# The second token weight kept in row order: no staging, no Pool copies, a stepped read in the matmul, and late z turns queued early

## Chip, cores, metric

One core of a Trainium2 chip. The time is the device time of one execution in microseconds (us), quoted as a median of several. This program runs on one core, so a run is marked slow by its time alone, when it lies over 1.5% above the fastest of its kernel. The granted clock is TensorE's clock as a share of full speed.

## The reference

Eight batches of 3008 tokens by 256 channels. An attention without softmax, a gate by `u`, and then a two-part mixer:

```python
scores = (1 / S) * (z @ z.T)                  # z: [8, 3008, 64]
attn   = np.maximum(scores, 0) ** 2
x      = u * (attn @ v)                       # [8, 3008, 256]
h      = np.maximum(x.T @ w_tok1, 0) @ w_tok2 # w_tok2: [256, 3008]
u2     = x + h.T
out    = u2 + np.maximum(u2 @ w_ch1, 0) @ w_ch2
```

## The kernel before

S = 3008 tokens are taken in six groups of QW = 512 (the last has 448: three full tiles of 128, and a rest of 64). Inside a group, partition p holds n = 4 neighbouring tokens (3 in the last group), so that the loads have long runs. All that is laid along the tokens inside the kernel (`uT`, `acc`, `xT`) therefore has the order "tile t, partition s", while the weight `w_tok2` comes from memory in the order "s, t". Before, Pool brings it into the kernel's order:

```python
def load_w_tok2(c):
    st = sb.tile([P, DT, QW], BF16, tag="h2", name="ws", bufs=ROOM["h2"])
    W = widths[c]
    nc.gpsimd.dma_start(out=st[:, :, :W], in_=...[:, :, c * QW:c * QW + W])
    ...
def order_w_tok2(c):
    ...
    for h in range(DT):
        nc.gpsimd.tensor_copy(
            w_tok2_sb[:, h, c * QW:c * QW + n * P].rearrange("p (t s) -> p t s", s=P),
            st[:, h, :n * P].rearrange("p (s t) -> p t s", t=n))
    if n * P < W:
        nc.gpsimd.tensor_copy(w_tok2_sb[:, :, c * QW + n * P:c * QW + W], st[:, :, n * P:W])
```

The matmul that uses it, and VectorE's addition behind it. The third argument of `matmul`, here the weight, is called the moving operand below, and a column is one of its elements in each partition, 512 or 448 in this kernel; its tile lies in SBUF. `h_ps` lies in PSUM, where this kernel puts the results of its matmuls, with room for 512 fp32 columns for each of two channel halves:

```python
def tok2(q, end):
    ...
    for dh in range(DT):
        for th in range(2):
            nc.tensor.matmul(
                h[:, dh, :W], st["a"][:, th, dh * P:(dh + 1) * P],
                w_tok2_sb[:, th, q * QW:q * QW + W], start=(th == 0), stop=(th == 1))
    def add(t):
        nc.vector.tensor_add(xT[:, :, :W], xT[:, :, :W], h[:, :, :W])
        ...
```

In each attention block VectorE squares the scores (`square`, one instruction for each pair of score tiles) and, at the end of a block, multiplies the two accumulator halves by `uT` (`gate`, one instruction for each half; this is the hand-over that frees the accumulators for TensorE). After the second gate the block's `xT` is turned by a DMA transpose into `x_sb`:

```python
def square(unit, view, t):
    nc.vector.tensor_mul(view, view, view)
    ...
def gate(blk, dh, t):
    ...
    nc.vector.tensor_mul(xT[:, dh, ...], acc[...], uT[:, :full, dh, :])
    ...
    if dh == DT - 1:
        push("sp", t, 1.25, 7.5, lambda t: turn_x(b, q, t), first=1)   # DMA transpose x_sb <- xT
```

The program is written by a scheduler that models the engines' times and decides in which order each engine's instructions are emitted. In the first batch the last two of six groups of `z` are doubled by VectorE and turned by TensorE in the middle of the first block:

```python
def turn_late_z(c):
    zr = double_first_z(c)
    ...
    turn_on_pe(zr, zp)
    ...
for c in range(GK, NG):
    at_group(c - GK + 1, lambda c=c: turn_late_z(c))
```

## Time and profile before

| | before |
|---|---|
| median of three runs | 1175.21 us (1170.55 to 1176.49) |
| profiled span, granted clock | 1168.6 us, 0.999 |
| TensorE busy, matmuls | 1159.7 us, 7049 |
| `h_ps` matmuls | 192, worth 40.6 us at the pace of the chain |
| Pool's 13 ordering copies | 9.0 us, once in the program |

How to read it: TensorE is busy for all but 9 us, so what counts of a matmul is its **pace**, the distance from one to the next in the chain. The lines of the profile stand in the prediction below.

### The profile page before, as it was taken

What the parts mean: (1) busy time and instruction counts of PE and PEld (TensorE: products, weight loads), DVE (VectorE), ACT (ScalarE), POOL (GpSimd) and SP (SyncE); (2) the same over time, 40 slices, a digit from 0 to 9 for tenths busy, and PEclk for the clock granted to TensorE, in tenths of its full rate; (3) what the DMA queues carried; (4) which work ended last, traced back from release to release, by engine and by line L of the source; (5) the groups of instructions that cost most, each with busy time, mean ns of one, the idle gap of its engine ahead of it and who ended that gap; (6) DMA issues with size and microseconds to landing.
All of it is one profiled execution on the core that took longest, in us unless ns stands there. A gap on an engine that the chain in (4) does not pass through costs nothing.

```text
span 1168.6 us, 17791 instructions
## 1 busy us (share of the span) xinstructions
PE 1159.7 (99%) x7049; PEld 630.0 (54%) x7049; DVE 541.8 (46%) x819; ACT 521.4 (45%) x650; POOL 158.3 (14%) x328
## 2 busy tenths in 40 slices
PE   9999999999999999999999999999999999999998
PEld 3334554655546555555555655465454655555666
DVE  5785653355333563435634355242552336512544
ACT  7877443244442363343524435344454344513221
POOL 4462001102012100120101210101201000000000
PEclk9999999999999999999999999999999999999999
DMA  9999737997497965896758986798667977632121
GB/s 166 186 157 197 173 92 149 162 190 132 117 167 152 168 132 134 145 181 147 145 131 163 166 152 125 138 186 156 122 141 140 187 145 151 121 100 58 50 82 64
DMA packets 472883, 165.57 MB, mean 142 GB/s; under 512 B 436640, under 2 KB 450528, under 8 KB 472800
## 3 DMA queue, kind: packets, MB, share of 16 engines
q1 hardware_dynamic: 444944, 131.74, 53.6%
q0 software_dynamic: 27344, 32.32, 19.8%
q8 instruction: 55, 0.90, 0.3%
q10 hardware_dynamic: 512, 0.38, 0.1%
q14 instruction: 28, 0.23, 0.1%
HBM read 65.40 MB, written 24.64 MB: 77 GB/s over the span
## 4 chain that ended last, share of the span: by engine, by line
PE 93%; DMA 3%; DVE 2%; POOL 1%; issue 1%; ACT 0%; SPq 0%; ACTq 0%; DVEq 0%; POOLq 0%
PE acc L533 39%; PE op L771 21%; PE hp L729 21%; PE sc L399 6%; PE a_ps L675 4%; PE h_ps L692 3%; DVE at L445 1%; DMA zT<-zr 1%; DMA ur<-in_u_dram 1%; DMA fl<-at 0%; DMA uT<-ur 0%; DMA zf<-in_z_dram 0%; DVE xT L628 0%; ACT at L437 0%; DVE xT L698 0%
## 5 line engine op out<-in xcount | busy, mean ns | idle before, releaser
L742 ACT ACTIVATE h2pre<-hp 128x1024 bf16<-128x1024 f32 (+1 forms) x191 | 191.0, 1006 | 364.5 <-PE hp L729 363.4
L533 PEld LDWEIGHTS <-v_sb 128*128 128x128 bf16 (+1 forms) x2304 | 209.6, 98 | 267.1 <-issue 65.1
L533 PE MATMUL acc<-at,v_sb 128*128 128x512 bf16 (+3 forms) x1464 | 350.7, 378 | 1.9 <-DVE xT L628 1.3
L437 ACT ACTIVATE at<-sc 128x1024 bf16<-128x1024 f32 (+1 forms) x284 | 272.0, 1024 | 159.4 <-PE sc L399 156.1
L445 DVE TENSOR_TENSOR at<-at 128x1024 bf16<-128x1024 bf16 (+1 forms) x284 | 200.7, 716 | 174.3 <-ACT at L437 174.1
L729 PE MATMUL hp<-xT,w_ch_sb 128*128 128x512 bf16 (+1 forms) x1152 | 266.7, 375 | 0.0
L771 PE MATMUL op<-w_ch_sb,h2pre 128*128 128x256 bf16 x2208 | 258.4, 273 | 0.3 <-DVE xT L698 0.2
L771 PEld LDWEIGHTS <-h2pre 128*128 128x128 bf16 x2208 | 215.9, 98 | 46.1 <-issue 0.5
L533 PE MATMUL acc<-fl,v_sb 128*128 128x512 bf16 (+1 forms) x840 | 199.9, 371 | 0.0
L729 PEld LDWEIGHTS <-w_ch_sb 128*128 128x128 bf16 x1152 | 112.7, 98 | 126.8 <-issue 0.2
L784 DVE TENSOR_TENSOR res<-op,u_sb 128x512 f32<-128x512 f32 x87 | 60.1, 691 | 206.5 <-PE op L771 206.5
L744 DVE TENSOR_SCALAR h2pre<-hp 128x1024 bf16<-128x1024 f32 (+1 forms) x97 | 117.3, 1209 | 52.4 <-PE hp L729 51.5
L628 DVE TENSOR_TENSOR xT<-acc,uT 128x512 bf16<-128x512 f32 (+1 forms) x96 | 63.2, 665 | 114.0 <-PE acc L533 113.6
L399 PE MATMUL sc<-zT 64*128 64x512 bf16 (+1 forms) x732 | 95.2, 361 | 0.3
L425 ACT ACTIVATE at<-sc 128x512 bf16<-128x512 f32 (+3 forms) x164 | 59.2, 446 | 67.7 <-PE sc L399 67.5
L125 POOL COPY zr<-zs 128x512 bf16<-128x512 bf16 x42 | 26.1, 623 | 399.6 <-DMA zT<-zr 393.9
L473 DVE TENSOR_TENSOR at<-at 128x512 bf16<-128x512 bf16 (+3 forms) x164 | 44.3, 324 | 59.2 <-ACT at L425 59.2
L399 PEld LDWEIGHTS <-zT 64*128 64x128 bf16 x732 | 31.2, 94 | 56.8 <-issue 39.8
L698 DVE TENSOR_TENSOR xT<-xT,h_ps 128x1024 bf16<-128x1024 bf16 (+1 forms) x48 | 55.6, 1191 | 6.4 <-PE h_ps L692 6.3
L168 POOL DMA_DIRECT2D v_sb<-in_v_dram x48 | 25.9, 545 | 143.7 <-PE acc L533 142.4
L675 PE MATMUL a_ps<-x_sb,w_tok_sb 128*128 128x256 bf16 x384 | 44.7, 273 | 0.0
L692 PE MATMUL h_ps<-w_tok_sb,a_sb 128*128 128x512 bf16 (+1 forms) x192 | 44.5, 374 | 0.1
(43 smaller groups left out, 209.9 us busy)
## 6 DMA issues: line engine op xcount, KB each, us to landing
out_dram<-res SPq DMA_DIRECT2D x87, 256.0 KB, 2.2
v_sb<-in_v_dram POOLq DMA_DIRECT2D x40, 256.0 KB, 4.9
ur<-in_u_dram POOLq DMA_DIRECT2D x40, 256.0 KB, 5.1
zs<-in_z_dram POOLq DMA_DIRECT2D x35, 64.0 KB, 4.4
at<-at SPq DMA_TRANSPOSE x123, 2.4
fl<-at SPq DMA_TRANSPOSE x105, 3.9
v_sb<-in_v_dram POOLq DMA_DIRECT2D x8, 192.0 KB, 6.3
ur<-in_u_dram POOLq DMA_DIRECT2D x8, 192.0 KB, 5.6
```

Source lines behind the costliest of these rows:

```text
L399: nc.tensor.matmul(sc[:, r, c0:c1], zT[h, k * P:(k + 1) * P], zT[h, q * QW + c0:q * QW + c1], start=True, stop=True)
L437: nc.scalar.activation(view, sv, ACT.Relu, scale=inv_S)
L445: nc.vector.tensor_mul(view, view, view)
L533: nc.tensor.matmul(o, vs[blk.b, g][rows, i, dh * P:(dh + 1) * P], rhs, start=first, stop=stop, skip_group_check=True)
L628: nc.vector.tensor_mul(xT[:, dh, :full * P].rearrange("p (t s) -> p t s", s=P), acc[:, :full * P].rearrange("p (t s) -> p t s", s=P), uT[: ...
L675: nc.tensor.matmul(st["a_ps"][:, th, :], w_tok1_sb[:, k, th * P:(th + 1) * P], x[:, :, i, :], start=(k == 0 and th == 0), stop=(k == KT - ...
L692: nc.tensor.matmul(h[:, dh, :W], st["a"][:, th, dh * P:(dh + 1) * P], w_tok2_sb[:, th, q * QW:q * QW + W], start=(th == 0), stop=(th == 1))
L729: nc.tensor.matmul(hp[:, r, :W], w_ch1_sb[:, dc, cc * P:(cc + 1) * P], xT[:, dc, :W], start=(dc == 0), stop=(dc == DT - 1))
L742: nc.scalar.activation(h2[:, :, :W], hp[:, :, :W], ACT.Relu)
L744: nc.vector.tensor_single_scalar(h2[:, :, :W], hp[:, :, :W], 0.0, AX.max)
L771: nc.tensor.matmul(op[:, i, :], h2, w_ch2_sb[:, cc, :], start=(cc == 0 and (i == 0 or apart)), stop=(cc == CHT - 1), skip_group_check=True)
L784: nc.vector.tensor_add(res.rearrange("p i (h d) -> p i h d", d=P), op.rearrange("p i (h d) -> p i h d", d=P), us[:, :, half * 2:half * 2 + ...
```

## The change

The intent: keep the weight as it comes, load it straight into its place, and let the matmul's moving operand pick every fourth element (every third in the last group). That drops the staging tiles and the copies. Because the 384 stepped columns and the rest of 64 don't form one regular pattern, the last group's matmul is split into 384 and 64 columns. Along with it the late `z` turns become pieces that are queued at the start and taken as soon as they are ready.

```diff
     def load_w_tok2(c):
-        st = sb.tile([P, DT, QW], BF16, tag="h2", name="ws", bufs=ROOM["h2"])
         W = widths[c]
         nc.gpsimd.dma_start(
-            out=st[:, :, :W],
+            out=w_tok2_sb[:, :, c * QW:c * QW + W],
             in_=...
-    def order_w_tok2(c):
-        ...                                   # the Pool copies shown above
@@ tok2
+                    a = st["a"][:, th, dh * P:(dh + 1) * P]
+                    w = w_tok2_sb[:, th, q * QW:q * QW + W]
                     nc.tensor.matmul(
-                        h[:, dh, :W], st["a"][:, th, dh * P:(dh + 1) * P],
-                        w_tok2_sb[:, th, q * QW:q * QW + W], start=(th == 0), stop=(th == 1))
+                        h[:, dh, :n * P].rearrange("p (t s) -> p t s", s=P), a,
+                        w[:, :n * P].rearrange("p (s t) -> p t s", t=n),
+                        start=(th == 0), stop=(th == 1), skip_group_check=True)
+                    if n * P < W:
+                        nc.tensor.matmul(
+                            h[:, dh, n * P:W], a, w[:, n * P:], start=False,
+                            stop=(th == 1), skip_group_check=True)
@@ late z
-    def turn_late_z(c):
-        ...
-    for c in range(GK, NG):
-        at_group(c - GK + 1, lambda c=c: turn_late_z(c))
+    def late_z(c, landed):
+        zr = []
+        def turn(end):
+            ...
+            turn_on_pe(zr[0], zp)
+            ...
+        cast = push("dve", landed, 0.42, 0.55, lambda t: zr.append(double_first_z(c)))
+        heads.append(Piece(0.23, [cast], turn, urgent=True))
...
     score_run(units[:2], 5.3)
+    late_z(4, 7.8)
+    late_z(5, 9.0)
```

More of the change, by code (lines that the diff above doesn't have):

```diff
@@ L45, with __init__ @@
 class Piece:
-    def __init__(self, cost, needs, fn, opens=False, closes=False, room=None):
+    def __init__(self, cost, needs, fn, opens=False, closes=False, room=None,
+                 urgent=False):
         self.cost, self.needs, self.fn = cost, needs, fn
         self.opens, self.closes, self.room = opens, closes, room
+        self.urgent = urgent
 @with_exitstack
@@ L205, in load_w_tok2 @@
     def load_w_tok2(c):
-        st = sb.tile([P, DT, QW], BF16, tag="h2", name="ws", bufs=ROOM["h2"])
         W = widths[c]
         nc.gpsimd.dma_start(
-            out=st[:, :, :W],
+            out=w_tok2_sb[:, :, c * QW:c * QW + W],
             in_=moe_w_tok2.rearrange("(tc t) s -> t tc s", t=P)[:, :, c * QW:c * QW + W])
-        ws[c] = st
-        live["h2"] += 1
         loading(LOAD)
-    def order_w_tok2(c):
-        st = ws.pop(c)
-        live["h2"] -= 1
-        W, n = widths[c], full_tiles[c]
-        for h in range(DT):
-            nc.gpsimd.tensor_copy(
-                w_tok2_sb[:, h, c * QW:c * QW + n * P].rearrange("p (t s) -> p t s", s=P),
-                st[:, h, :n * P].rearrange("p (s t) -> p t s", t=n))
-        if n * P < W:
-            nc.gpsimd.tensor_copy(
-                w_tok2_sb[:, :, c * QW + n * P:c * QW + W], st[:, :, n * P:W])
     def load_w_ch(part):
@@ L237, in load_w_ch @@
         loading(LOAD * 1.5)
-    zTs, vs, urs, uTs, xTs, xs, ws = {}, {}, {}, {}, {}, {}, {}
+    zTs, vs, urs, uTs, xTs, xs = {}, {}, {}, {}, {}, {}
     attn = {}
@@ L689, in tok2 @@
             h = psum.tile([P, DT, QW], F32, tag="ps", name="h_ps", bufs=3)
+            n = full_tiles[q]
             for dh in range(DT):
                 for th in range(2):
+                    a = st["a"][:, th, dh * P:(dh + 1) * P]
+                    w = w_tok2_sb[:, th, q * QW:q * QW + W]
                     nc.tensor.matmul(
-                        h[:, dh, :W], st["a"][:, th, dh * P:(dh + 1) * P],
-                        w_tok2_sb[:, th, q * QW:q * QW + W], start=(th == 0), stop=(th == 1))
+                        h[:, dh, :n * P].rearrange("p (t s) -> p t s", s=P), a,
[5 more added lines that the diff above has]
+                            stop=(th == 1), skip_group_check=True)
             def add(t):
@@ L938 @@
                              lambda b=b, c=c: load_v(b + 1, c))
-    def turn_late_z(c):
-        zr = double_first_z(c)
-        free["dve"] = max(free["dve"], pe[0]) + 0.45
-        while all(d.t is None for d in ring):
-            run_engines(next_op()[0][0])
-        begin = max(free["dve"] + 0.1, min(d.t for d in ring if d.t is not None))
-        take_slot()
-        begin, end = on_pe(max(pe[0], begin), "full", 0.23)
-        zp = psum.tile([P, GK, P], F32, tag="ps", name="zp", bufs=3)
-        turn_on_pe(zr, zp)
-        turned[0, c] = Done()
-        ring.append(push(
-            "dve", end + 0.1, 0.66, 0.8,
-            lambda t: nc.vector.tensor_copy(zTs[0][:, c * GK:c * GK + GK, :], zp[:]),
-            first=1, done=turned[0, c]))
-    for c in range(GK, NG):
-        at_group(c - GK + 1, lambda c=c: turn_late_z(c))
+    def late_z(c, landed):
+        zr = []
+        def turn(end):
+            take_slot()
+            zp = psum.tile([P, GK, P], F32, tag="ps", name="zp", bufs=3)
+            turn_on_pe(zr[0], zp)
+            turned[0, c] = Done()
+            ring.append(push(
+                "dve", end + 0.2, 0.66, 0.8,
+                lambda t: nc.vector.tensor_copy(zTs[0][:, c * GK:c * GK + GK, :], zp[:]),
+                first=1, done=turned[0, c]))
+        cast = push("dve", landed, 0.42, 0.55, lambda t: zr.append(double_first_z(c)))
+        heads.append(Piece(0.23, [cast], turn, urgent=True))
     at_group(3, lambda: turn_u(0, 0))
@@ L969 @@
     items += [lambda c=c: load_w_tok1(c) for c in range(NG)]
-    first_tok2 = len(items)
     items += [lambda c=c: load_w_tok2(c) for c in range(NG)]
@@ L975 @@
         at_group(n, item)
-        if 0 <= k - first_tok2 < NG:
-            at_group(n + 4, lambda c=k - first_tok2: order_w_tok2(c))
     per_batch = 0.87 * NQ * (2 + CHT // 2) + 1.35 * 4 * NQ
@@ L1037 @@
             pick, n_now, ts = "scores", now, t
+        elif tm <= t + NOW and pieces[0].urgent:
+            pick = "mixer"
         elif hold and opened[0] is not None and tm <= t + NOW and pieces is opened[0]:
@@ L1075 @@
         else:
-            budget -= pieces[0].cost
+            if not pieces[0].urgent:
+                budget -= pieces[0].cost
             do_piece(tm, pieces)
```

## The prediction

> **What bounds the kernel now.** I read the page first, its busy times and its chain of waits, then the groups by line, then the stretches where the chain leaves TensorE.
>
> ```profile
> PE 1159.7 (99%) x7049; PEld 630.0 (54%) x7049; DVE 541.8 (46%) x819; ACT 521.4 (45%) x650; POOL 158.3 (14%) x328
> PE 93%; DMA 3%; DVE 2%; POOL 1%; issue 1%; ACT 0%; SPq 0%; ACTq 0%; DVEq 0%; POOLq 0%
> PE acc L533 39%; PE op L771 21%; PE hp L729 21%; PE sc L399 6%; PE a_ps L675 4%; PE h_ps L692 3%; DVE at L445 1%; DMA zT<-zr 1%; DMA ur<-in_u_dram 1%; DMA fl<-at 0%; DMA uT<-ur 0%; DMA zf<-in_z_dram 0%; DVE xT L628 0%; ACT at L437 0%; DVE xT L698 0%
> ```
>
> TensorE is busy 99% of 1168.6 us and carries 93% of the chain. So every nanosecond put into a matmul is paid in full, and a nanosecond taken from Pool or VectorE is worth something only in the few places where TensorE waits for them. The granted clock is 0.999, so no throttle is in play. The operation that the change touches is h_ps, 3% of the span. The groups by line:
>
> ```profile
> L692 PE MATMUL h_ps<-w_tok_sb,a_sb 128*128 128x512 bf16 (+1 forms) x192 | 44.5, 374 | 0.1
> L698 DVE TENSOR_TENSOR xT<-xT,h_ps 128x1024 bf16<-128x1024 bf16 (+1 forms) x48 | 55.6, 1191 | 6.4 <-PE h_ps L692 6.3
> L220 POOL COPY w_tok_sb<-ws 128x512 bf16<-128x512 bf16 (+1 forms) x12 | 8.7, 755 | 1.0 <-DMA ws<-in_moe_w_tok_dram 1.0
> L125 POOL COPY zr<-zs 128x512 bf16<-128x512 bf16 x42 | 26.1, 623 | 399.6 <-DMA zT<-zr 393.9 <-DMA zs<-in_z_dram 5.5
> ```
>
> 374 ns is the latency of one matmul, with its overlap. What it costs is its pace, which the chain in order of time gives:
>
> ```profile
> 115.86 2.59 PE h_ps L692 x12
> 263.43 0.76 PE h_ps L692 x4
> ```
>
> So 2.59/12 = 0.216 us for 512 columns and 0.76/4 = 0.19 us for 448. All of h_ps is 160 x 0.216 + 32 x 0.19 = 40.6 us.
>
> Pool is idle most of the time, but its copies are not quite harmless. In the only stretch where L220 runs (67.2 to 80.2 us) the chain goes through VectorE; first the chain, then the group in that stretch, then the timeline:
>
> ```profile
> 67.61 11.41 DVE at L445 x11
> 79.02 0.24 issue
> 79.26 1.74 DVE at L445
> 81.00 0.61 DVE xT L628
> ```
> ```profile
> L445 DVE TENSOR_TENSOR at<-at x13: 612/1062/2387, 65.7 to 79.3; 128x1024 bf16<-128x1024 bf16 x8, 128x896 bf16<-128x896 bf16 x5
> ```
> ```profile
> 81.66 2.73 PE L533 MATMUL acc<-at,v_sb 128*128 128x448 bf16 x14 [0.72 <-DVE xT L628]
> ```
>
> L445, the square, has a median of 692 ns over the whole run and 1062 ns here, once 2387 ns. VectorE falls behind, the gate that frees the accumulator comes late, and TensorE waits for it, but only 0.72 us. That is the whole visible price of the staging.
>
> The start is the other place. Two z groups are cast by VectorE and turned by TensorE in the middle of the first block (first fence, the timeline), and the block's end hangs on a transfer (second fence, the chain):
>
> ```profile
> 11.11 0.23 PEld L149 LDWEIGHTS <-zr 128*128 128x128 bf16 x4 [0.93 <-DVE zr L143]
> 11.12 0.40 PE L149 MATMUL zp<-ident,zr 128*128 128x128 bf16 x4 [0.43 <-DVE zr L143]
> 15.53 0.40 PE L149 MATMUL zp<-ident,zr 128*128 128x128 bf16 x4 [0.25 <-DVE zr L143]
> ```
> ```profile
> 11.67 6.98 DMA ur<-in_u_dram
> 18.65 0.02 issue
> 18.66 5.78 DMA uT<-ur
> 24.45 0.03 issue
> 24.48 0.02 DVEq L628
> 24.50 0.04 issue
> 24.54 0.70 DVE xT L628
> 25.24 0.04 issue
> 25.29 0.81 PE acc L533 x3
> ```
>
> [...] The new read steps 4 bf16 = 8 bytes (3 = 6 bytes in the last group)[...]. No matmul of this trace steps its moving operand between neighbouring elements[...]. Pool reads with this very step in L220: the two 128x384 copies took 521 ns each, where the unit-step 128x512 copies of L125 have a median of 613 and the 128x128 copies of L749 a mean of 296; a line through those two gives about 507 ns at 384 columns. So no penalty on Pool, at a lower rate of elements. [...] the 692 ns squares become 1062 beside L220. [...]
>
> **The change, part by part.**
>
> Removed, Pool copies: 13 copies, 9.0 us of Pool, once in the program and not per batch. Worth on the path: the 0.72 us wait at 81.66. Estimate -0.7 us. The six loads stay, with the same bytes and the same runs; only the target differs.
>
> Removed, staging tiles: six buffers of the pool of eight, all during the first batch, when the mixer that shares them hasn't begun. No wait on them is seen. Zero.
>
> Moved, the late z turns: the casts are queued at the start and the turns are taken as soon as they are ready. The waits that vanish are 0.43 + 0.25 = 0.68 us. TensorE is idle 1.51 us between 5.6 and 25.3 us (19.70 less 18.19 busy). But the block can't hand over before uT has landed at 24.45 and the gate has run; TensorE's own last matmuls of that block ended near 24.3, so both arrive together. What TensorE gains earlier it mostly waits for at 25.29. I take half of the 0.68, -0.3 us.
>
> Added, the split tail: in the last group 448 columns become 384 + 64, so 4 more pairs of weight load and matmul per batch, 32 in all. The four turning pairs above go at 0.23/4 = 57 ns a pair with 128 columns, so a pair with 64 columns costs at most about that, against 64/448 x 190 = 27 ns of the stream that it takes over: +30 ns x 32 = +1.0 us.
>
> Changed, the moving read: 192 matmuls, the 160 full ones and 32 of 384 columns. If the stride is free, 0. If it halves the rate, these 192 take twice their 160 x 0.216 + 32 x 0.163 = 39.8 us, so +39.8 us, none of it hidden, since TensorE is the bound; VectorE's add behind each group of four (1.19 us) would then be shorter than the 1.73 us of the matmuls and hide.
>
> Sum with a free stride: -0.7 - 0.3 + 1.0 + 0 = 0.0 us, so 1175 us, the median of before.
>
> **Rivals.** First, the stride costs. A rate of one half gives 1175 + 40 = 1215 us, slower by 3.4%; a loss of a quarter of the rate (a third more time) gives 1188. For it speaks that TensorE takes 512 elements in 0.216 us, 2.4 in a nanosecond, twice what the line through the copies of Pool gives (1.2)[...]. [...] I give full cost 12% and partial cost 10%.
>
> Second, the start is worth more. If ScalarE, no longer starved (it waits 4.3 us for scores between 5 and 26 us), runs ahead so far that the second block goes without gaps, all of the 1.51 us and some of the filling matmuls come back, and the copies' end gives a little more: 1172 us. Against it stands uT at 24.45, which the change doesn't touch[...].
>
> Third, the order of emission shifts. The program orders its pieces by a model of the engines' times, and an earlier start can reorder score runs and mixer pieces in later batches. Each wait that can arise is under a microsecond; I allow 3 us either way, the same size as the spread of before's runs (1170.55 to 1176.49).
>
> **Range and chances.** With a free stride (78%) the sum of the small terms and the spread gives 1168 to 1180. Partial cost reaches from 1180 to 1200, full cost lies near 1215. A range of 1166 to 1190 holds the first case and half of the second. Faster by over 2% would need 23 us out of a kernel whose TensorE is idle 9 us in all: 1%. Slower by over 2% starts at 1199, so it takes the full cost or nearly: 16%. Within 2%: 83%.
>
> **What would show it right or wrong.** The pace of h_ps in the chain: 2.59 us for 12 means that the stride is free, 5.2 that it is halved. Squares near 67 to 80 us back at 0.69 us, and the 0.72 us wait at the gate gone. The first block's hand-over still near 25 us, with uT as its releaser. Matmuls up by 32, to 7081 or a few others by the filling ones. The prediction is wrong if h_ps's matmuls keep TensorE longer than 42 us, or if the hand-over of the first block moves by over 2 us.

## The result, and the profile after

The change costs 52 us. Before had a median of 1173.02 us (1170.55 to 1176.49, 4 runs), after 1221.68 us (1221.67 to 1225.04, 4 runs); the ratio is 1.042, interval 1.0382 to 1.0457, outside the predicted range of 1166 to 1190. All ratios in this document compare fast runs of the same rounds, so they are not quite the ratio of the medians. All results are correct unless said otherwise.

The page of after, its busy times and the chain by line:

```profile
PE 1203.4 (99%) x7081; PEld 635.4 (52%) x7081; DVE 540.0 (44%) x819; ACT 521.6 (43%) x650; POOL 150.5 (12%) x315
...
PE acc L521 39%; PE op L767 20%; PE hp L725 20%; PE h_ps L683 7%; PE sc L387 6%; PE a_ps L663 4%; DMA fl<-at 1%; DMA ur<-in_u_dram 1%; DMA zf<-in_z_dram 0%; DMA uT<-ur 0%; ACT at L425 0%; POOL v_sb L170 0%; SPq L480 0%; DVE xT L616 0%; SPq L628 0%
```

The profiled span went from 1168.6 to 1219.9 us, by 51.3. TensorE's busy time went up by 43.7 us (1159.7 to 1203.4) and its idle time by 7.6 (8.9 to 16.5). `h_ps` has gone from 3% to 7% of the span, and `DMA fl<-at` from 0% to 1%. So there are **two costs**: most of it is work, some of it is waiting. The matmuls are 7081, the predicted 32 more, and Pool has its 13 copies less.

The work first. The chain of after in order of time; the columns are start, length, what, how many:

```profile
127.23 5.42 PE h_ps L683 x12
...
139.05 2.06 PE h_ps L683 x5
141.11 0.03 PE h_ps L688
141.13 0.25 PE h_ps L683
```

Twelve matmuls of 512 columns took 2.59 us before and take 5.42 us now, and further on twenty take 9.03 us: 0.4515 us each instead of 0.216. The last group gives the other two prices: 0.25 us for the 384 columns and 0.03 us for the split-off 64. All of `h_ps` is now 160 x 0.4515 + 32 x 0.25 + 32 x 0.03 = 81.2 us against 40.6, so +40.6 us. The groups by form show it too, though there the duration of one (before: 374 ns for both forms together) hides that it is a pace:

```profile
L683 PE MATMUL h_ps<-w_tok_sb,a_sb 128*128 128x512 bf16 x160 | 75.5, 628 | 0.0
L683 PE MATMUL h_ps<-w_tok_sb,a_sb 128*128 128x384 bf16 x32 | 10.2, 418 | 0.0
```

Now the waiting. The timeline of after; the brackets give the idle time before and what ended it:

```profile
25.04 1.02 PE L521 MATMUL acc<-at,v_sb 128*128 128x512 bf16 x4 [1.36 <-DVE xT L616]
...
112.73 2.86 ACT L425 ACTIVATE at<-sc 128x1024 bf16<-128x1024 f32 x3 [12.34 <-DMA fl<-at]
113.81 1.86 PE L663 MATMUL a_ps<-x_sb,w_tok_sb 128*128 128x256 bf16 x8 [8.74 <-ACT at L425]
```

At 112.73 ScalarE has waited 12.34 us for the transposes of score tiles (`fl<-at`), and behind it TensorE has waited 8.74 us. Nothing of this kind is in before, whose longest wait of TensorE is 1.2 us, at the start. A second price goes with the wait, the clock. In the table by stretches of after (columns: stretch, length, granted clock, DMA share, GB/s) it is 0.50 from 110 to 120 us, at the end of the wait and after it, where before has 1.00,

```profile
30.00:35.00 5.00, 1.00 1.23 148
110.00:120.00 10.00, 0.50 1.23 244
```

and the chain's 40 `a_ps` matmuls behind the wait take 6.57 us where before's take 4.47. That is 8.7 + 2.1 = 10.8 us for wait and clock together. (One long wait isn't needed for it: in the profile of late_only below the clock was 0.81 from 105 to 110 us and 0.51 from 110 to 115 us, though no wait of TensorE there was longer than 1.3 us.)

The first line of that table points to where it begins. In before the transfers run faster in the same stretch:

```profile
30.00:35.00 5.00, 1.00 1.19 214
```

And just ahead of it VectorE's order differs, at the first block's hand-over. VectorE's timeline, after and then before:

```profile
24.29 0.69 DVE L616 TENSOR_TENSOR xT<-acc,uT 128x512 bf16<-128x512 f32 x1 [1.25 <-DMA uT<-ur]
24.90 0.68 DVE L433 TENSOR_TENSOR at<-at 128x1024 bf16<-128x1024 bf16 x1
25.50 0.68 DVE L616 TENSOR_TENSOR xT<-acc,uT 128x512 bf16<-128x512 f32 x1
```
```profile
24.54 1.29 DVE L628 TENSOR_TENSOR xT<-acc,uT 128x512 bf16<-128x512 f32 x2 [0.24 <-DMA uT<-ur]
```

Before runs the two gates one after the other; after has one square between them, because the other place of the late `z` turns changed the order in which the scheduler emitted VectorE's work. The second gate ends 0.35 us later, and the DMA transpose `x_sb<-xT` that it releases is issued 1.45 us after Pool's waiting load of `u` (26.21 and 24.76 us) instead of 0.86 us (25.86 and 25.00). Whether so small a thing can be the cause is what the experiments had to show.

### The profile page after: what moved, and what is told of

It is laid out like the page before. It is cut to its first block, busy times and chain, and to the rows that moved or that the text cites. A ratio compares the mean times of both kernels' runs of the same rounds, so it can differ in the third digit from the quotient of the medians.

```text
span 1219.9 us, 17833 instructions
## 1 busy us (share of the span) xinstructions
PE 1203.4 (99%) x7081; PEld 635.4 (52%) x7081; DVE 540.0 (44%) x819; ACT 521.6 (43%) x650; POOL 150.5 (12%) x315
## 4 chain that ended last, share of the span: by engine, by line
PE 96%; DMA 2%; DVE 0%; ACT 0%; POOL 0%; SPq 0%; issue 0%; DVEq 0%; ACTq 0%
PE acc L521 39%; PE op L767 20%; PE hp L725 20%; PE h_ps L683 7%; PE sc L387 6%; PE a_ps L663 4%; DMA fl<-at 1%; DMA ur<-in_u_dram 1%; DMA zf<-in_z_dram 0%; DMA uT<-ur 0%; ACT at L425 0%; POOL v_sb L170 0%; SPq L480 0%; DVE xT L616 0%; SPq L628 0%
## 5 line engine op out<-in xcount | busy, mean ns | idle before, releaser
L433 DVE TENSOR_TENSOR at<-at 128x1024 bf16<-128x1024 bf16 (+1 forms) x284 | 195.4, 693 | 195.0 <-ACT at L425 194.4
L683 PE MATMUL h_ps<-w_tok_sb,a_sb 128*128 128x512 bf16 (+1 forms) x192 | 84.8, 593 | 0.0
L663 PE MATMUL a_ps<-x_sb,w_tok_sb 128*128 128x256 bf16 x384 | 47.6, 283 | 8.7 <-ACT at L425 8.7
L663 PEld LDWEIGHTS <-w_tok_sb 128*128 128x128 bf16 x384 | 38.8, 101 | 18.6 <-issue 9.9
```

What stands on the lines that cost most here:

```text
L663: nc.tensor.matmul(st["a_ps"][:, th, :], w_tok1_sb[:, k, th * P:(th + 1) * P], x[:, :, i, :], start=(k == 0 and th == 0), stop=(k == KT - ...
L683: nc.tensor.matmul(h[:, dh, :n * P].rearrange("p (t s) -> p t s", s=P), a, w[:, :n * P].rearrange("p (s t) -> p t s", t=n), start=(th == 0 ...
```

## The experiments

Runs of one group below shared a chip and the runs of before on it: 1171.54 us (20 runs), 1171.44 (39), 1171.86 (27) and 1171.76 (23) in the four groups. Two of the theories of the stepped read speak of units of memory: each unit touched costs a fixed time, where the unit is a word of 8 bytes (one column each at step 4) or a line of 16 bytes (two columns each at step 4). A third lets the price grow with the distance between neighbouring elements.

### First group: the parts, and the step

**late_only**: before with the new late `z` turns alone; staging, copies and unit-step matmul stay.

```diff
-    for c in range(GK, NG):
-        at_group(c - GK + 1, lambda c=c: turn_late_z(c))
...
+    late_z(4, 7.8)
+    late_z(5, 9.0)
```

> The kernel before plus the late z part of the change alone; staging, Pool copies and the unit-step read as before. If the 8.7 us wait near 105 us comes from the shifted start, it shows here too and the time is 1178 to 1185 us. If it comes from the loads that are no longer spaced by Pool's copies, it is absent and the time is within 2 us of before. In either case the first block still hands over near 25 us, with uT as its releaser.

Measured 1184.04 us (1171.04 to 1188.04, 17 runs), ratio 1.0083 (1.0058 to 1.0108). So this part, predicted at -0.3 us, costs some 12 us in the median and about 10 by the ratio. The interval leaves out 1, here and in the other runs with this loss below. The runs are not all alike: a few lie at 1171 to 1174. The profiled one was of these (1174.61 us): its longest wait of this kind was 1.3 us and its transfers between 30 and 35 us ran at 205 GB/s. The loss thus comes in most executions, not in all. Before has the reverse: of its 39 executions in the second group, four lie at 1179 to 1180 us and one at 1186.

**step1**: after with a unit step, the split kept. The result is wrong (relative error 0.78), since the weight isn't in the kernel's order.

```diff
-                        w[:, :n * P].rearrange("p (s t) -> p t s", t=n),
+                        w[:, :n * P].rearrange("p (t s) -> p t s", s=P),
```

> The changed kernel with one thing undone: the matmuls of the second token weight read unit step (384 + 64 columns in the last group kept, result wrong on purpose). Theory A, the step of the moving read costs the time: pace of h_ps back from 0.452 to 0.216 us per 512 columns, some 39 us less, about 1180 us. Rival, the split form (two matmuls, a reshaped output) or the direct load is what costs: the pace stays above 0.3 us and the time near 1220. A second question rides on it: TensorE's 8.7 us wait near 105 us. If it comes from the timing of transfers in the first batch, it stays, since nothing before 120 us differs; time then near 1182 rather than 1172.

Measured 1181.37 us (1179.57 to 1185.56, 4 runs), ratio 1.0093 (1.0065 to 1.0121). Its chain:

```profile
125.04 2.59 PE h_ps L683 x12
```

The pace of before is back, to the last digit, with direct load and split in place; the 40 us are the step and nothing else. What remains, 10 us, fits the wait near 105 us (7.0 us here) and the half clock behind it (0.50 from 110 to 115 us). The split costs nothing: 0.16 + 0.03 us for 384 and 64 columns are the 0.19 us of the old 448.

**step2** and **step8**: after with steps of 2 and of 8 elements in the moving operand (wrong; the output view is changed with it to keep the same shape).

```diff
-                        h[:, dh, :n * P].rearrange("p (t s) -> p t s", s=P), a,
-                        w[:, :n * P].rearrange("p (s t) -> p t s", t=n),
+                        h[:, dh, :n * P].rearrange("p (t s) -> p t s", t=2), a,   # step8: t=8
+                        w[:, :n * P].rearrange("p (s t) -> p t s", t=2),          # step8: t=8
```

> The changed kernel with a step of 2 elements (4 bytes) in all six groups, result wrong on purpose. Theory A1, every 8 bytes of SBUF that the matmul touches cost about 0.88 ns (fits step 4: 0.882 ns a column, and step 3: 3 words for 4 columns, 0.66 ns against 0.65 measured): two columns per word, 0.44 ns a column, so 0.216 to 0.226 us for 512 columns, nearly free, about 1181 us. Theory A2, any step other than 1 halves the rate: 0.45 us and about 1220 us. [...]

> The changed kernel with a step of 8 elements (16 bytes), result wrong on purpose. Theory A1, a price per 8-byte word: no dearer than step 4, 0.45 us for 512 columns, time near 1220 us (the last group's 384 columns go from 0.25 to 0.34 us). Theory A4, a price per 16-byte line or a read that slows with the distance: clearly dearer, 0.6 to 0.9 us for 512 columns, 1250 to 1300 us.

One run each, 1188.95 and 1339.37 us, of unknown state; the paces are what counts. The chain of step2, then of step8:

```profile
132.96 2.70 PE h_ps L683 x12
```
```profile
132.42 10.79 PE h_ps L683 x12
```

Step 2 gives 0.225 us, step 4 gave 0.4515 and step 8 gives 0.899. If a word of 8 bytes were the unit, step 8 would cost no more than step 4, one word per column in both; it costs twice as much. That theory falls. A line of 16 bytes fits, and so does a price by distance, since from 2 to 8 both double with the step.

The whole time of step8 holds something more. Its clock fell to half during the stepped matmuls themselves (132.4 to 143.2 us), while TensorE was busy without a gap: the four `acc` matmuls just ahead of them took 0.97 us, the four just behind 1.71 us. The table by stretches:

```profile
138.00:143.00 5.00, 0.50 0.46 105
```

The pace was the same at both clocks: the next four matmuls, all at half clock, took 3.58 us, 0.895 us each. But the ten matmuls after them (`acc`, unit step) took 4.27 us instead of 2.16. step16 below shows the same (0.97 and 1.71 us), and the mean clock of both profiles is 0.94; at step 4 (the profiles of stride_only and after_together) it stayed at 0.999.

### Second group: each part alone, and another place for the step

**stride_only**: before with direct load and stepped matmul, no Pool copies, and the old late `z` turns.

> The kernel before plus the second token weight's part alone: direct load, stepped read, no Pool copies; the late z turns as before. Stepped read: 40 us, so 1213 us. If the 8.7 us wait near 105 us comes from the missing copies, it is here too: 1222. The 0.72 us wait at the gate near 81 us must be gone either way, and the squares near 67 to 80 us back at 0.69 us.

Its edit is the first two parts of the diff of the change. Measured 1211.54 us (1208.87 to 1217.8, 4 runs), ratio 1.0338 (1.0293 to 1.0384). `h_ps` takes 5.42 us for 12, there is no long wait near 105 us, and the transfers between 30 and 35 us run at 217 GB/s. The median is 40.1 us above before's.

**after_again**: after, unchanged, on this chip.

> The changed kernel once more, on the same chip as these three. 1222 us again, with the wait near 105 us in its profile; if that wait is a matter of chance in the transfers, it is shorter or absent here and the time spreads by several us.

1223.56 us (1214.06 to 1226.44, 4 runs), ratio 1.0419 (1.0363 to 1.0475), 52.1 us over before's median. Its profile has the wait again (9.5 us), and 83 GB/s between 30 and 35 us. The parts add up: 40.1 (stride_only) + 12.5 (late_only, 1184.04 - 1171.54) = 52.6.

**dve_reads**: before with the direct load and without the copies, but the matmul reads with a unit step, and VectorE's addition takes the step when it reads PSUM.

```diff
-                nc.vector.tensor_add(xT[:, :, :W], xT[:, :, :W], h[:, :, :W])
+                xv = xT[:, :, :n * P].rearrange("p h (t s) -> p h t s", s=P)
+                nc.vector.tensor_add(
+                    xv, xv, h[:, :, :n * P].rearrange("p h (s t) -> p h t s", t=n))
+                if n * P < W:
+                    nc.vector.tensor_add(
+                        xT[:, :, n * P:W], xT[:, :, n * P:W], h[:, :, n * P:W])
```

> The kernel before with the direct load and no Pool copies, but the matmul reads unit step and writes in row order; VectorE's add takes the step instead, reading PSUM 16 bytes apart. Correct result. Theory: TensorE's pace back to 0.216 us; the add grows from 1.19 us to at most 2.4 us, on an engine that is idle half the time, so little of it shows: 1171 to 1178 us. Rival: the add becomes the bound behind each token stage, since six adds of 2 us follow six pieces of 0.86 us: up to 7 us a batch, 1200 us and more.

1171.21 us (1168.53 to 1185.91, 19 runs of 20), ratio 1.0001 (0.9983 to 1.0019). The addition of full groups, by form:

```profile
L686 DVE TENSOR_TENSOR xT<-xT,h_ps 128x1024 bf16<-128x1024 bf16 x40 | 47.3, 1214 | 6.3 <-PE h_ps L678 6.3
```

Its mean of 1214 ns is that of before for the same form, although the fp32 elements it reads now lie 16 bytes apart; the growth to at most 2.4 us didn't come. So the copies and the staging can go for nothing, if VectorE takes the step and not TensorE. No gain shows either: the time is that of before, within an interval of about 2 us to each side, so the 0.7 us that the copies were predicted to cost can't be seen in it.

**dve_reads_late**: the same on top of after, so with the new late `z` turns.

> The changed kernel (late z turns included) with the same move of the step to VectorE's add. If the late z turns or the changed timing of loads make the 8.7 us wait near 105 us, it is 8 to 11 us slower than dve_reads; if not, within 2 us of it.

1182.61 us (1169.12 to 1186.31, 17 runs of 20), ratio 1.0063 (1.0032 to 1.0094). In its profile the wait is 10.0 us and the transfers run at 133 GB/s. It tells again that the late turns cost their time without any stepped matmul: 11.4 us between the medians, about 7 by the ratios.

### Third group: lines against distance; two guesses about the wait

**step16**: as step8, with t=16.

> The changed kernel with a step of 16 elements (32 bytes), result wrong on purpose. Steps 2, 3, 4 and 8 took 0.439, 0.651, 0.882 and 1.756 ns a column, in proportion to the step. Theory L, a price of 1.76 ns for each 16-byte line touched: step 16 touches no more lines than step 8, so 0.90 us for 512 columns again and about 1340 us. Rival D, a price in proportion to the distance walked: 3.5 ns a column, 1.8 us for 512 columns and about 1500 us.

Its output is wrong, which doesn't matter for the time. One run, 1338.05 us. Its chain:

```profile
129.24 11.01 PE h_ps L683 x12
```

0.9175 us for 512 columns, 2% more than at step 8, where a price by distance asked for twice as much. At steps 8 and 16 each column has a line of 16 bytes to itself, so the **line** is the unit by these paces:

| step (bf16) | columns per 16-byte line | lines for the columns | measured us | ns per line |
|---|---|---|---|---|
| 1 | 8 | 64 (512) | 0.216 | 3.38 |
| 2 | 4 | 128 (512) | 0.225 | 1.76 |
| 3 | 8/3 | 144 (384) | 0.25 | 1.74 |
| 4 | 2 | 256 (512) | 0.4515 | 1.76 |
| 8 | 1 | 512 (512) | 0.899 | 1.76 |
| 16 | 1 | 512 (512) | 0.9175 | 1.79 |

At step 1 a line has 8 columns, and the 512 columns take 0.422 ns each (0.216 us / 512). An estimate from these paces: if a matmul takes the longer of 0.422 ns a column and 1.76 ns a line, a step costs nothing from 1.76 / 0.422 = 4.2 columns a line on. Step 2, with 4, was measured 4% slower than step 1 (0.225 us); step 4, with 2, took more than double (0.4515 us).

**late_turn_later**: dve_reads_late with one transpose of `u` (for the fourth block) asked for three score groups later.

```diff
-                at_group(base + q * NG + 5, lambda m=m: turn_u(m // NQ, m % NQ))
+                at_group(base + q * NG + (8 if m == 3 else 5),
+                         lambda m=m: turn_u(m // NQ, m % NQ))
```

> dve_reads_late with one thing moved: the DMA transpose of the fourth u block is issued three steps later, so that it no longer runs at 28 to 31 us among the loads of v and of the first token weight, where the runs with the long wait moved 70 to 150 GB/s against 205 to 217 in the others. Theory, that collision starts the backlog: the rate between 30 and 35 us is back above 200, the wait of TensorE near 105 us is under 2 us, median 1170 to 1174. Rival, the backlog comes of the early start in general: 1182 to 1186 as before.

1183.81 us (1170.08 to 1187.42, 20 runs), ratio 1.009 (1.0072 to 1.0107); the wait is still there, 11.6 us, with transfers at 89 GB/s. The theory that this transpose collides with the loads falls.

**late_loads_later**: dve_reads_late with the loads of the weights asked for three groups later.

```diff
+        if k >= NG:
+            n += 3
         at_group(n, item)
```

> dve_reads_late with the loads of the token and channel weights each asked three steps later, the transposes as they were. Theory, the crowd of loads behind the collision matters: fewer loads at 30 to 45 us, the wait near 105 us shorter, median under 1176. Rival, the transposes suffer from whatever loads are there, and these now come later, nearer to 105 us: no better than 1184, perhaps worse.

1183.8 us (1169.37 to 1185.77, 7 runs of 8), ratio 1.0068 (1.0026 to 1.011). No gain either: three groups later for the weights' loads don't help.

### Fourth group: one square, moved

**gates_together**: dve_reads_late, where the square that stands between the two gates of the first block is emitted behind the second. One instruction of VectorE changes its place; nothing else.

```diff
     def square(unit, view, t):
-        nc.vector.tensor_mul(view, view, view)
+        if held_back:
+            held_back.append(view)
+        else:
+            nc.vector.tensor_mul(view, view, view)
@@ gate
+        if (b, q, dh) == (0, 0, 0):
+            held_back.append(None)
...
+        if (b, q, dh) == (0, 0, 1):
+            for w in held_back[1:]:
+                nc.vector.tensor_mul(w, w, w)
+            held_back.clear()
```

> dve_reads_late with two VectorE instructions swapped and nothing else (every other engine's order is the same): the one square that stands between the two gates of the first block goes behind them, so the first x transpose starts 0.85 us after Pool's waiting u load instead of 1.45 us, as in every kernel without the late z turns. Theory, that offset against the burst of v loads decides whether transfers stall between 30 and 35 us: rate there 200 GB/s or more, no long wait near 105 us, median 1169 to 1172, with few runs above 1178. Rival, another consequence of the late z turns: 1183 to 1185 as before.

1170.66 us (1168.37 to 1182.51, 20 runs), ratio 0.9992 (0.9973 to 1.0012), where dve_reads_late had 1182.61 (on another chip, with before at 1171.44 there and 1171.76 here). In the traces of the two every engine but VectorE has its instructions in the same order, TensorE's weight loads standing for its matmuls, of which some records are missing. VectorE's timeline and the table by stretches:

```profile
24.46 1.29 DVE L622 TENSOR_TENSOR xT<-acc,uT 128x512 bf16<-128x512 f32 x2 [0.53 <-DMA uT<-ur]
```
```profile
30.00:35.00 5.00, 1.00 1.19 221
```

The gates are together, the transfers run at before's rate, and the longest wait of this kind is 0.4 us. Four of the 20 runs still lie at 1177 to 1183 us.

**gates_apart**: the reverse. dve_reads, which has before's late `z` turns and is as fast as before, with the second gate emitted behind the next square.

```diff
     def square(unit, view, t):
         nc.vector.tensor_mul(view, view, view)
+        while held_back:
+            held_back.pop()()
@@ gate
+        if (b, q, dh) == (0, 0, 1):
+            held_back.append(product)      # the gate's tensor_mul
+        else:
+            product()
```

> The converse: dve_reads (no late z turns) with one square moved between the two gates of the first block and nothing else. Theory: the offset becomes 1.45 us, the rate between 30 and 35 us falls to 70 to 150 GB/s in most runs, TensorE waits 7 to 15 us near 105 us, median 1180 to 1185. Rival: no change, 1171.

1187.25 us (1184.13 to 1188.52, 4 runs), ratio 1.0095 (1.0059 to 1.0131). The medians of this kernel and of all runs of before are 15.5 us apart; by the ratio, against the runs of the same rounds, it is 11 us. VectorE's timeline and the table by stretches:

```profile
24.88 0.68 DVE L618 TENSOR_TENSOR xT<-acc,uT 128x512 bf16<-128x512 f32 x1
25.48 0.68 DVE L432 TENSOR_TENSOR at<-at 128x1024 bf16<-128x1024 bf16 x1
26.08 0.68 DVE L618 TENSOR_TENSOR xT<-acc,uT 128x512 bf16<-128x512 f32 x1
```
```profile
30.00:35.00 5.00, 1.00 2.37 107
```

The wait near 105 us is there, 14.3 us long, in a kernel with the old `z` turns, and again no other engine's order differs from that of dve_reads. The order of these two VectorE instructions alone brings it and takes it away, in most executions.

**after_together**: after with the same swap.

> The changed kernel itself with the same swap of two VectorE instructions. If the account is the stepped read (40 us) plus the stalled transfers (10 to 12 us), this is 1210 to 1212 us, with no wait near 105 us. If the swap does nothing, 1222.

1211.6 us (1209.93 to 1212.98, 4 runs), ratio 1.0305 (1.0264 to 1.0347); no wait over 1.5 us, 217 GB/s, and `h_ps` at 5.42 us for 12. What is left of the change is the stepped read.

## Why the prediction was wrong, by its own steps

**"If the stride is free, 0"** is the step that failed, with the 78% put on it. It cost 40.6 us by the paces, +40.1 us in stride_only with the copies' gain in it. The prediction's rival had the size (+39.8 us) and gave it 12%. The reasoning behind the chance has three weak places:

- The 78% were the author's estimate, and that a step of 8 bytes is free for a moving operand was not shown: no matmul of before steps it. Measured, two columns on a 16-byte line ran at 48% of the rate of the unit step (0.216 / 0.4515), and four at 96% (0.216 / 0.225).
- It looked at Pool's stepped copies, where the line through the copies gave 1.2 elements in a nanosecond, and found no penalty. But the two copies that it read had step 3, not 4, and at that step TensorE itself takes 384 columns in 0.25 us, 1.5 in a nanosecond. Reads at 1.2 can't show a limit that lies at 1.5, even if they had the same price. The prediction named the difference between the two rates as what spoke for the rival, and still gave it 12%.
- It priced the rival as a guessed share of the rate (a half, a quarter). What the runs show from step 2 on is a price per line, 1.74 to 1.79 ns; "half" came out right because the step was 4, which is luck.

**The late z turns, -0.3 us**, cost +12 us in the median, 7 to 10 by the ratios of late_only and dve_reads_late. The prediction was right on the hand-over: it stayed near 25 us (25.29 before, 25.04 after), with `uT` as releaser, and the earlier start of TensorE went into a wait of 1.36 us at it. It was wrong that nothing else could follow. The third rival had "the order of emission shifts" and allowed 3 us, because "each wait that can arise is under a microsecond". What arose was a wait of 8.7 us and a clock of 0.50 after it. That term was mis-sized because it looked at waits between engines and not at what a shifted release does to the transfers.

**The split tail, +1.0 us**, cost nothing: 0.16 + 0.03 us in step1 are the old 0.19. The estimate took a pair of 128 columns at the start of the program (57 ns) as the price of one of 64 in a dense stream, where it took 30 ns.

**Pool's copies, -0.7 us**, were as predicted in what they slow: the squares between 66 and 82 us are back at a median of 0.65 us in after and 0.68 in stride_only (they were at 1.06), and the 0.72 us wait at 81.66 is gone. Whether that made the program 0.7 us faster is below what the runs resolve. The 32 more matmuls were as predicted too.

**What stays open.** That the gates' order in the first block sets the wait near 105 us is shown in both directions. The way from one to the other is not. Where the square stands between the gates the transpose `x_sb<-xT` is issued 0.6 us later behind Pool's load of `u`, and the transfers between 30 and 35 us move 71 to 148 GB/s in every profile with the long wait, instead of 205 to 221 in every profile without it; the wait then is for the transposes of scores. (late_only's profile is one without it, at 205 GB/s and with the later transpose, so the order sets the odds and not each execution.) Whether it is that offset that makes the transfers slower, and how, why it does so in most executions and not in all, and how the backlog lives on for 70 us, no trace shows; two guesses (another transpose, the weights' loads) fell.

## What to carry to other kernels

Where TensorE is the bound, keep the moving operand dense in SBUF and put a change of order into an engine with room: VectorE read PSUM with a step of four elements in the same 1214 ns as without, while the matmul paid 0.24 us for every 512 columns. Count the 16-byte lines that a stepped operand touches and compare their price (about 1.76 ns each here) with the time of the matmul (0.216 us for 512 columns), instead of asking whether a step is allowed. And after any change of emission order compare the transfer rate by stretches and the order of each engine around the first hand-overs; one square in another place cost here about a quarter of what the stepped read did.
